# The recurrent layers' inputs and outputs kept on the chip instead of passed through transposed DRAM tensors

## The chip, the cores and the metric

One core of one Trainium2 chip runs the whole program. Its engines, as the profile names them, are PE (TensorE matmuls; PEld are its weight loads), DVE (VectorE), ACT (ScalarE), POOL (GpSimd) and SP (SyncE, which here only issues DMA transfers). The metric is the device time of one launch in microseconds (us), lower is better.

## The reference

Four layers with residuals over x of 2048 rows by 576 columns. Layers 1 and 3 (A) are dilated sliding window attention; layers 2 and 4 (B) are a recurrent attention with a memory of 8 rows that is handed from one segment of 32 rows to the next.

```
x = x + A(layernorm(x)); x = x + B(layernorm(x), mem0)
x = x + A(layernorm(x)); x = x + B(layernorm(x), mem0)

A: qkv = x @ wqkv (32 heads of 18); logits over the rows s, s-2, ..., s-14; softmax; @ wo
B: for each of 64 segments: h = [mem (8 rows), x segment (32 rows)]
     q, k, v = h @ Wq, Wk, Wv          (32 heads of 128)
     o = softmax(q k^T * scale, masked) v;  o = o @ Wo
     mem = o[:8]; output rows = o[8:]
```

## The kernel before

Activations are held transposed: 576 columns on 128 partitions in five chunks, rows along the free axis. Layer A works on tiles of T = 64 rows (32 tiles per layer, `a_tile`), layer B on segments of 32 rows. The two B layers advance together: step t (`b_step`) computes segment t of layer 2 (lane 0) and segment t - 6 of layer 4 (lane 1) in one tile hT of 96 columns, 80 of them used: 32 rows of lane 0, 2 x 8 rows of memory, 32 rows of lane 1. There are 70 steps, and two steps use up one A tile of layer 1 and one of layer 3.

A step on PE: projections q and k (L728/L730, eleven groups of up to three heads), v (L759, three blocks of 32 rows, two halves of 20 matmuls each), scores in two kinds, m (memory rows) and x (segment rows) (L790/L800), probabilities times v (L817 for m, L850 for x), output projection into the PSUM tile psY (L874, eight pieces of 20 matmuls). The memory rows of psY go at once into the next step's hT (`mem_out`, L893 to L895). The x rows of step t are projected one step later, together with the memory rows of step t + 1.

An A tile on PE: layernorm sums (L402), qkv in 15 blocks of 5 matmuls (L479), logits (L528), probabilities spread over the columns (L552: 16 matmuls, then 4 more into the same PSUM tile once it is empty), output in 5 blocks of 5 (L587). A block of A's weights is loaded from DRAM into one of six `ring` buffers (L423), 40 blocks in two steps.

PSUM: three tiles r for everything narrow, one tile o4 (spread and probabilities times v), one psY.

How data passed between the layers in the kernel before: the normalised A output (xnb) was stored by SP to xn2T or xn4T (L611), and per step a 32 row piece of each was loaded into hT (L704). The x rows of psY were copied to stg (L905), stored per lane to d2T or d4T (L911), and later loaded as dl (L451, L621) beside the residual x1T or x3T (L450, L620), added on DVE (L456 for layer 3's input, L625 for the final output), and for the output transposed on PE (L634) and stored (L645).

The order of the work is set by a planner (`_Plan.run`): each operation has engines it may run on, an estimated duration, a priority (lower first) and buffers it acquires; whenever an engine is free in the planner's clock it takes the ready operation of lowest priority number. The result is one fixed order of instructions per engine. Each engine executes its own in that order, waiting where a semaphore says so; SP issues its transfers in order too, so that a transfer which waits holds all behind it.

Of the kernel before, what the change touches and what calls it, by code (L numbers as in the profile page):

```python
# [16 lines left out]
P = 128  # L17
# [177 lines left out]
class _K:  # L195
# [37 lines left out]
    def setup(self):  # L233
# [5 lines left out]
        NT, NSEG = self.NT, self.NSEG  # L239
        self.x1T = dp.tile([P, NT, 5, T], F32, name="x1T")  # L240
        self.x3T = dp.tile([P, NT, 5, T], F32, name="x3T")
        self.xnT = [dp.tile([P, NSEG, 6, SEG], BF16, name=f"xn{l}T") for l in (2, 4)]
        self.dT = [dp.tile([P, NSEG, 5, SEG], F32, name=f"d{l}T") for l in (2, 4)]
# [113 lines left out]
        tiles("stg", 2, [P, 2, 5, SEG], F32)  # L357
        tiles("nmx", 4, [P, 8], F32)
        tiles("sum", 4, [P, 8], F32)
        tiles("xT", 3, [P, 5, T], F32)  # L360
        tiles("dl", 1, [P, NS, 5, SEG], F32)
# [14 lines left out]
        tiles("xnb", 2, [P, NS, 6, SEG], zero=True)  # L376
# [49 lines left out]
    def a_tile(self, layer, j, dep, due, span):  # L426
# [6 lines left out]
        xT = pl.buf("xT")  # L433
        if layer == 1:
            x0, ps = pl.buf("x0"), pl.buf("r")
            a = pl.op("SP", 0.5, lambda e: nc.sync.dma_start(out=x0.t[0:T, 0:D], in_=self.A_x[0, j * T:(j + 1) * T, :]),
                      pr(0), [dep], acq=[x0])

            def tr(e, ps=ps):
                for c in range(5):  # L440
                    nc.tensor.matmul(ps.t[:, c * T:(c + 1) * T], lhsT=x0.t[:, c * P:(c + 1) * P], rhs=self.ident[:, 0:T],
                                     start=True, stop=True)
            b = pl.op("PE", 0.16, tr, pr(0.04), [a], acq=[ps, xT], uses=[x0])
            o_x = pl.op(AD_, _evac(320), lambda e, ps=ps: self.copy(e, xT.t[:], ps.t[:, 0:5 * T].rearrange("p (c t) -> p c t", c=5)),
                        pr(0.05), [b], uses=[ps, xT])
        else:
            dl = pl.buf("dl")

            def ld(e):
                nc.sync.dma_start(out=xT.t[:], in_=self.x1T[:, j])  # L450
                nc.sync.dma_start(out=dl.t[:], in_=self.dT[0][:, NS * j:NS * j + NS])  # L451
            a = pl.op("SP", 1.0, ld, pr(0), [dep, self.x1_stored[j], *self.d_stored[0][NS * j:NS * j + NS]], acq=[xT, dl])

            def add(e):
                xv = xT.t[:].rearrange("p c (s n) -> p c s n", n=SEG)
                nc.vector.tensor_tensor(out=xv, in0=xv, in1=dl.t[:].rearrange("p s c n -> p c s n"), op=ALU.add)  # L456
            o_x = pl.op("DVE", 0.52, add, pr(0.05), [a], uses=[xT, dl])
# [138 lines left out]
        xnb = pl.buf("xnb")  # L596

        def wr2(e, m, rstd):
# [5 lines left out]
            for o, i, bc in views:  # L604
# [6 lines left out]
        o = pl.op("SP", 0.5, lambda e: nc.sync.dma_start(out=self.xnT[lane][:, NS * j:NS * j + NS], in_=xnb.t[:]),  # L611
                  pr(0.95), [o], uses=[xnb])
        self.xn_stored[lane][j] = o

    def finish_out(self, j, prio):
        nc, pl = self.nc, self.pl
        xT, dl, xb, ot = pl.buf("xT"), pl.buf("dl"), pl.buf("fin"), pl.buf("ot")

        def ld(e):
            nc.sync.dma_start(out=xT.t[:], in_=self.x3T[:, j])  # L620
            nc.sync.dma_start(out=dl.t[:], in_=self.dT[1][:, NS * j:NS * j + NS])  # L621
        a = pl.op("SP", 1.0, ld, prio, [self.x3_stored[j], *self.d_stored[1][NS * j:NS * j + NS]], acq=[xT, dl])

        def add(e):
            nc.vector.tensor_tensor(out=xb.t[:, 0:5 * T].rearrange("p (c s n) -> p c s n", c=5, n=SEG),  # L625
                                    in0=xT.t[:].rearrange("p c (s n) -> p c s n", n=SEG),
                                    in1=dl.t[:].rearrange("p s c n -> p c s n"), op=ALU.add)
        a = pl.op("DVE", 0.52, add, prio, [a], acq=[xb], uses=[xT, dl])
# [66 lines left out]
    def load_x(self, t):  # L695

        nc, pl = self.nc, self.pl
        hT = pl.buf("hT")
        self.hT[t] = hT
        segs = [(l, self.lane_seg(t, l)) for l in range(2) if self.lane_seg(t, l) is not None]  # L700

        def ld(e):
            for l, s in segs:
                nc.sync.dma_start(out=hT.t[:, :, XC[l]:XC[l] + SEG], in_=self.xnT[l][:, s])  # L704
        o = pl.op("SP", 0.5 * len(segs), ld, t - 0.42, [self.xn_stored[l][s // NS] for l, s in segs] + [self.qk_op.get(t - 1)],
                  acq=[hT])
        self.x_in[t] = o
        for l, s in segs:
            if s == 0:
                m0 = MC + l * NM  # L710
                o = pl.op("DVE", 0.2, lambda e, m0=m0: nc.vector.tensor_copy(out=hT.t[:, :, m0:m0 + NM], in_=self.mem0T[:]),
                          t - 0.4, [o], uses=[hT])
                self.mem_in.setdefault(t, []).append(o)

    def qk(self, t, g, prio):
# [16 lines left out]
        o = pl.op("PE", 0.358 * n, mm, prio, [self.x_in[t], *self.mem_in[t]], acq=[ps, sb], uses=[hT], tmin=TW[0])  # L732
# [9 lines left out]
    def vpass(self, t, b, prio):  # L742
# [5 lines left out]
        gate = pl.op("NONE", 0.0, None, prio, [self.x_in[t]], acq=[V])  # L748
        for r in range(2):
# [10 lines left out]
            o = pl.op("PE", 1.08, mm, prio, [self.x_in[t], gate] + (self.mem_in[t] if b == 1 else []), acq=[ps], uses=[hT, V],  # L760
# [121 lines left out]
    def mem_out(self, t, dep, prio):  # L882
# [13 lines left out]
        o = pl.op("DVE", 0.56, cp, prio, [dep, self.x_in[t + 1]], uses=[psY, hT])  # L896
        self.mem_in.setdefault(t + 1, []).append(o)

    def x_out(self, t, dep, prio):

        nc, pl, psY = self.nc, self.pl, self.psY
        if t < 0:
            return
        st = pl.buf("stg")
        o = pl.op(AD_, _evac(320), lambda e: self.copy(e, st.t[:].rearrange("p l c n -> p c l n"),  # L905
                                                       psY.t[:, :, 16:W80].rearrange("p c (l n) -> p c l n", l=2)),
                  prio, [dep], acq=[st], uses=[psY])
        for lane in range(2):
            s = self.lane_seg(t, lane)
            if s is not None:  # L910
                self.d_stored[lane][s] = pl.op("SP", 0.5, lambda e, lane=lane, s=s: nc.sync.dma_start(out=self.dT[lane][:, s], in_=st.t[:, lane]),  # L911
                                               prio, [o], uses=[st])
# [29 lines left out]
    def trace(self):  # L942
# [3 lines left out]
        self.xn_stored = [[None] * NT, [None] * NT]  # L946
        self.d_stored = [[None] * NSEG, [None] * NSEG]
        self.hT, self.x_in, self.mem_in, self.qk_op, self.V, self.v_ev, self.e_ = {}, {}, {}, {}, {}, {}, {}
        nl = 0
        for t in range(self.nsteps):  # L950
            while nl < NT and NS * nl <= t + LEAD:
                self.a_tile(1, nl, self.qk_op.get(t - 1), NS * nl - 0.5, 3.0)
                nl += 1
            for lane in range(2):
                s = self.lane_seg(t - 2, lane) if t >= 2 else None
                if s is not None and s % NS == NS - 1:
                    j = s // NS
                    if lane == 0:
                        self.a_tile(3, j, None, NS * j + self.dly - 0.5, 2.2)
                    else:  # L960
                        self.finish_out(j, t + 1.5)
            if t == 0:
# [75 lines left out]
```

## Time and profile before

| | before |
|---|---|
| time, median of 3 runs (range) | 2752.93 us (2750.78 to 2760.56) |
| the profiled execution: own time, span | 2747.74 us, 2745.9 us |
| granted TensorE clock, mean | 0.98 |
| busy: PE, DVE, ACT, POOL | 2388.5, 1927.1, 936.5, 980.0 us |
| DMA queue of SP: share of 16 engines | 35.9% (275.02 MB) |
| first PE instruction after the start of the span | 103.9 us (it waits for the first load of x) |

The span is cut by the profile in busy time and idle time of each engine, and idle time is put down to what ended it. A row such as "PE r L479 <- DMA ring<-wA_blk: 42.6, 57, 2.1" reads: PE, before matmuls of line 479 that write a tile r, sat idle 42.6 us in total in 57 places, at most 2.1 us, until a transfer into ring had landed.

### The profile page before, as it was taken

To read this page: it belongs to the slowest core of one execution; us is meant where nothing else is said; L and a number is where in the kernel's file an instruction comes from. 1 tells how busy PE (TensorE), PEld (TensorE's weight loads), DVE (VectorE), ACT (ScalarE), POOL (GpSimd) and SP (SyncE) were. 2 spreads that over 40 slices of the span, in tenths; PEclk is the share of its full clock that TensorE was granted. 3 is DMA by queue.
4 is the path that set the end of the run, shared out by engine and by line. 5 is a ranking of instruction groups with operands and counts; after the bars stand their busy time and mean duration, and the time that the engine had idled before them with its cause. 6 is when DMAs were issued, how large, how long until landed. Compare 5 with 4: busy or idle time off the path is not lost. (4 is left out here: it accounts for less than half of the span.)

```text
span 2745.9 us, 159278 instructions
## 1 busy us (share of the span) xinstructions
PE 2388.5 (87%) x73360; PEld 2001.8 (73%) x73360; DVE 1927.1 (70%) x4021; ACT 936.5 (34%) x2070; POOL 980.0 (36%) x1177
## 2 busy tenths in 40 slices
PE   0289999999989988999998989899999999999998
PEld 0177777777777777777777777777777777777777
DVE  1266777777777777777777777777777777776665
ACT  0023334333333333333333333333333333333322
POOL 3231333433434443334343344443433433332110
PEclk9999999999999999999999999999999999999999
DMA  7722433344443344334444434443334444432210
GB/s 253 198 74 65 117 103 104 108 115 118 117 126 110 108 124 115 104 98 122 123 115 123 125 100 117 126 113 109 110 108 127 111 123 127 118 86 79 64 30 19
DMA packets 368642, 304.08 MB, mean 111 GB/s; under 512 B 146788, under 2 KB 364452, under 8 KB 366436
## 3 DMA queue, kind: packets, MB, share of 16 engines
q1 hardware_dynamic: 364724, 275.02, 35.9%
q0 software_dynamic: 3248, 18.88, 2.0%
q8 instruction: 573, 9.39, 1.5%
q14 instruction: 97, 0.79, 0.1%
HBM read 260.88 MB, written 32.90 MB: 107 GB/s over the span
## 5 line engine op out<-in xcount | busy, mean ns | idle before, releaser
L728 PE MATMUL r<-hT,wq 128*128 128x80 bf16 x8960 | 694.5, 202 | 11.5 <-DVE V L225 6.2
L728 PE MATMUL r<-hT,wk 128*128 128x80 bf16 x8960 | 693.9, 202 | 0.0
L728 PEld LDWEIGHTS <-wq 128*128 128x128 bf16 x8960 | 463.8, 100 | 48.7 <-issue 45.2
L874 PE MATMUL psY<-OT,wo 128*128 128x80 bf16 (+1 forms) x11360 | 482.4, 208 | 18.7 <-ACT OT L223 9.4
L225 DVE CAST qk<-r 128x480 bf16<-128x480 f32 (+1 forms) x506 | 324.4, 642 | 242.2 <-PE r L730 219.6
L759 PE MATMUL r<-wv,hT 128*32 128x512 bf16 x6720 | 447.3, 384 | 51.6 <-ACT em L673 21.1
L874 PEld LDWEIGHTS <-wo 128*128 128x128 bf16 x11360 | 460.2, 104 | 30.3 <-issue 23.9
L728 PEld LDWEIGHTS <-wk 128*128 128x128 bf16 x8960 | 465.3, 100 | 0.1
L730 PE MATMUL r<-hT,wk_r 128*128 128x80 bf16 x2240 | 452.7, 202 | 0.0
L730 PE MATMUL r<-hT,wq_r 128*128 128x80 bf16 x2240 | 452.6, 202 | 0.0
L230 POOL TENSOR_TENSOR big<-qT,kT 128x1024 bf16<-128x1024 bf16 (+1 forms) x192 | 332.0, 1737 | 186.6 <-ACT kT L223 178.4
L759 PEld LDWEIGHTS <-hT 128*32 128x32 bf16 x8400 | 208.9, 97 | 229.8 <-issue 73.4
L230 POOL TENSOR_TENSOR ex<-ex,sum 128x384 bf16<-128x384 bf16 x140 | 117.0, 836 | 536.1 <-DVE sum L681 482.5
L479 PE MATMUL r<-xn,ring 128*128 128x64 bf16 x4800 | 235.3, 196 | 62.5 <-DMA ring<-wA_blk 50.5
L479 PEld LDWEIGHTS <-ring 128*128 128x128 bf16 x4800 | 179.7, 99 | 123.1 <-DMA ring<-wA_blk 76.1
L223 ACT ACTIVATE V<-r 128x512 bf16<-128x512 f32 x269 | 160.8, 598 | 289.3 <-PE r L759 289.0
L230 POOL TENSOR_TENSOR big<-big 128x1280 bf16<-128x1280 bf16 (+1 forms) x84 | 187.5, 2232 | 130.5 <-DVE big L230 128.5
L730 PEld LDWEIGHTS <-wq_r 128*128 128x128 bf16 x2240 | 224.1, 100 | 1.4 <-issue 1.3
L730 PEld LDWEIGHTS <-wk_r 128*128 128x128 bf16 x2240 | 224.1, 100 | 0.0
L223 ACT ACTIVATE qk<-r 128x480 bf16<-128x480 f32 (+1 forms) x264 | 146.7, 558 | 204.0 <-PE r L730 197.0
L223 ACT ACTIVATE OT<-o 128x512 bf16<-128x512 f32 (+1 forms) x299 | 143.1, 500 | 154.7 <-DVE OT L225 92.2
L223 ACT ACTIVATE big<-o 128x512 bf16<-128x512 f32 x220 | 125.1, 596 | 168.1 <-PE o L552 112.8
(137 smaller groups left out, 3643.7 us busy)
## 6 DMA issues: line engine op xcount, KB each, us to landing
ring<-wA_blk SPq DMA_DIRECT2D x1280, 160.0 KB, 3.2
x1T<-xT SPq DMA_DIRECT2D x32, 160.0 KB, 2.7
d2T<-stg SPq DMA_DIRECT2D x64, 80.0 KB, 3.2
xT<-x1T SPq DMA_DIRECT2D x32, 160.0 KB, 3.7
dl<-d2T SPq DMA_DIRECT2D x32, 160.0 KB, 4.3
x3T<-xT SPq DMA_DIRECT2D x32, 160.0 KB, 3.2
d4T<-stg SPq DMA_DIRECT2D x64, 80.0 KB, 3.0
xT<-x3T SPq DMA_DIRECT2D x32, 160.0 KB, 3.8
```

Source lines behind the costliest of these rows:

```text
L223: nc.scalar.activation(out=out, in_=in_, func=ACT.Copy, scale=1.0 if scale is None else scale)
L225: (nc.vector if e == "DVE" else nc.gpsimd).tensor_copy(out=out, in_=in_)
L230: (self.nc.vector if e == "DVE" else self.nc.gpsimd).tensor_tensor(out=out, in0=in0, in1=in1, op=op)
L479: nc.tensor.matmul(ps.t[:, c * T:(c + 1) * T], lhsT=w.t[:, kc, :], rhs=xn.t[:, kc, :], start=(kc == 0), stop=(kc == 4))
L728: nc.tensor.matmul(pv[:, hh, wi, :], lhsT=wt[:, kc, h * P:(h + 1) * P], rhs=hT.t[:, kc, 0:W80], start=(kc == 0), stop=False)
L730: nc.tensor.matmul(pv[:, hh, wi, :], lhsT=wr[:, (h % 16) * P:(h % 16 + 1) * P], rhs=hT.t[:, 4 + h // 16, 0:W80], start=False, stop=True)
L759: nc.tensor.matmul(ps.t[c * 32:(c + 1) * 32, :], lhsT=l, rhs=w, start=(kc == 0), stop=(kc == 4))
L874: nc.tensor.matmul(psY.t[:, mb, c0:], lhsT=self.wo[:, w0:w0 + P], rhs=self.OT[:, h, c0:], start=(h == 0 and mb == 0), stop=(h == NH - 1 an ...
```

## The change

Four edits, and a new order that follows from them.

- `load_x`: no transfer. hT's x columns are copied from xnb on POOL or DVE (128 copies of 128 x 192 elements). xnb has its own two buffers per layer.
- `x_out`: no copy to stg and no store. DVE adds psY's rows of a lane straight to the residual tile, which `residual` has loaded before: in place for layer 3's input (tile x3), into `fin` for the final output (tile x5 is loaded, fin is written).
- `a_tile` for layer 3 and `finish_out` begin with those tiles and load nothing; the two DVE additions of 64 rows fall away.
- Priorities: A tiles of layer 1 are due at 2*nl - 0.6 with a spread of 3.5 (was - 0.5, 3.0), those of layer 3 at 2*j + 4.8 with 1.0 (was 2*j + 5.5 with 2.2).

```
 load_x:
-        def ld(e):
-            for l, s in segs:
-                nc.sync.dma_start(out=hT.t[:, :, XC[l]:XC[l] + SEG], in_=self.xnT[l][:, s])
+        gate = pl.op("NONE", 0.0, None, t - 0.42, [self.qk_op.get(t - 1)], acq=[hT])
+            xnb, dep = self.xn_ready[l][s // NS]
+            self.x_in[t][l] = pl.op(("POOL", "DVE"), (0.45, 0.2),
+                                    lambda e, ...: self.copy(e, hT.t[:, :, XC[l]:XC[l] + SEG], xnb.t[:, s % NS]),
+                                    t - 0.42, [dep, gate], uses=[hT, xnb])
 new:
+    def residual(self, lane, j, dep, prio):
+        b = pl.buf(("x3", "x5")[lane])
+        xb = pl.buf("fin") if lane == 1 else None
+        src = (self.x1T, self.x3T)[lane]
+        o = pl.op("SP", 0.5, lambda e: nc.sync.dma_start(out=b.t[:], in_=src[:, j]), prio, ...
 x_out:
-        st = pl.buf("stg")
-        o = pl.op(AD_, _evac(320), lambda e: self.copy(e, st.t[:]..., psY.t[:, :, 16:W80]...), ...)
-                self.d_stored[lane][s] = pl.op("SP", 0.5, lambda e, ...: nc.sync.dma_start(out=self.dT[lane][:, s], in_=st.t[:, lane]), ...)
+                x = xT.t[:, :, w]
+                o = x if xb is None else xb.t[:, 0:5 * T]...[:, :, w]
+                nc.vector.tensor_tensor(out=o, in0=x, in1=psY.t[:, :, c0:c0 + SEG], op=ALU.add)
 trace:
-                self.a_tile(1, nl, self.qk_op.get(t - 1), NS * nl - 0.5, 3.0)
+                self.a_tile(1, nl, self.qk_op.get(t - 1), NS * nl - 0.6, 3.5)
-                        self.a_tile(3, j, None, NS * j + self.dly - 0.5, 2.2)
+                        self.a_tile(3, j, None, NS * j + self.dly - 1.2, 1.0)
+            for lane in range(2):
+                s = self.lane_seg(t, lane)
+                if s is not None and s % NS == 0:
+                    self.residual(lane, s // NS, self.qk_op.get(t - 1), t + 0.3)
```

Instructions by engine, before and after: PE 146722 rows both times, line for line the same number of matmuls; SP 1894 and 1510 issues (gone are 128 stores of d2T/d4T, 64 loads of dl, 64 stores and 128 loads of xn2T/xn4T); DVE 4023 and 4096; ACT 2072 and 2050; POOL 1182 and 1255. The planner also gives some operations to another engine: the widest addition of an A tile (128 x 1280 elements) goes 58 times to POOL and 6 times to DVE before, 5 and 59 times after; 90 evacuations of q and k go from DVE to ACT.

Both orders repeat every two steps through the middle of the program, here called the even and the odd step of a pair. PE in the order after, odd step, from the end of its output projection: 16 spread matmuls (L542), one transpose of `fin` (L622), the first q/k group of the next step, three weight blocks of an A tile (L469), then probabilities times v (L841, into o4), one block, the two halves of v, the last 4 spread matmuls, five blocks and more. Even step: m scores, x scores, layernorm sums (L401), half of v, logits (L518), half of v, two q/k groups, 16 spread matmuls, A's output (L577), one q/k group, 4 spread matmuls. In the order before, the even step has m scores, x scores and both halves of v in a row, and its spread stands among the output projection: 16 spread matmuls, 20 of L874, layernorm sums, 4 spread matmuls, probabilities times v (L817).

SP's queue at the turn from an even to an odd step. Ahead of the fence: in the order before, x3T, xT, dl and xn2T stand between the ring loads that follow an A tile's output and the next ones.

```order
L423 DMA ring_335<-wA_blk 128x640
L423 DMA ring_336<-wA_blk 128x640
L593 DMA x3T<-xT_303 128x320
L450 DMA xT_302<-x1T 128x320
L451 DMA dl_305<-d2T 128x320
L611 DMA xn2T<-xnb_325 128x384
L423 DMA ring_331<-wA_blk 128x640
```

The same turn in the order after, where x_298 is a tile x3 and x_300 the tile x5:

```order
L422 DMA ring_334<-wA_blk 128x640
L609 DMA x_298<-x1T 128x320
L422 DMA ring_335<-wA_blk 128x640
L422 DMA ring_330<-wA_blk 128x640
L422 DMA ring_332<-wA_blk 128x640
L422 DMA ring_331<-wA_blk 128x640
L422 DMA ring_333<-wA_blk 128x640
L422 DMA ring_334<-wA_blk 128x640
L609 DMA x_300<-x3T 128x320
L422 DMA ring_335<-wA_blk 128x640
```

Two residual loads are left at this turn, six ring loads apart.

DVE in the even step, at the softmax of the first scores (nmx is a negated maximum, sum a row sum, em the m probabilities, st the layernorm statistics), before:

```order
L670 TENSOR_REDUCE nmx_294<-r_340 128x4
L671 TENSOR_TENSOR r_340<-r_340,nmx_294 128x320
L670 TENSOR_REDUCE nmx_295<-r_342 128x8
L671 TENSOR_TENSOR r_342<-r_342,nmx_295 128x384
L680 TENSOR_REDUCE sum_298<-em_268 128x4
L681 RECIPROCAL sum_298<-sum_298 128x4
L683 TENSOR_TENSOR em_268<-em_268,sum_298 128x4x80
```

And after:

```order
L658 TENSOR_REDUCE nmx_288<-r_339 128x4
L659 TENSOR_TENSOR r_339<-r_339,nmx_288 128x320
L407 TENSOR_SCALAR st_304<-r_340 128x64
L408 TENSOR_TENSOR st_304<-st_304 128x64
L409 SCALAR_TENSOR_TENSOR st_304<-r_340,st_304 128x64
L668 TENSOR_REDUCE sum_292<-em_264 128x4
L669 RECIPROCAL sum_292<-sum_292 128x4
L671 TENSOR_TENSOR em_264<-em_264,sum_292 128x4x80
L658 TENSOR_REDUCE nmx_289<-r_341 128x8
L659 TENSOR_TENSOR r_341<-r_341,nmx_289 128x384
```

Three statistics of a layernorm and the m normalisation now stand ahead of the x scores' maximum, which before followed the m maximum directly.

DVE at the end of the odd step's output projection, after (`big` is the A tile's spread tile, OT the B heads' output):

```order
L884 CAST hT_260<-psY 128x4x16
L885 CAST hT_260<-psY 64x16
L886 CAST hT_260<-psY 64x16
L225 CAST big_314<-o_342 128x32x16 x2
L906 TENSOR_TENSOR x_299<-x_299,psY 128x5x32
L230 TENSOR_TENSOR big_314<-big_314,vT_309 128x1024 x2
L225 CAST OT<-o_342 128x2x4x64
L906 TENSOR_TENSOR fin_327<-x_300,psY 128x5x32
```

The memory copies come first, then two of the four evacuations of the spread tile, and the two new additions (L906) stand between products of A and an evacuation of B.

More of the change, by code (lines that the diff above doesn't have):

```diff
@@ L375, in setup @@
         tiles("oT", 1, [P, 5, T])
-        tiles("xnb", 2, [P, NS, 6, SEG], zero=True)
+        tiles("xnb1", 2, [P, NS, 6, SEG], zero=True)
+        tiles("xnb3", 2, [P, NS, 6, SEG], zero=True)
         tiles("fin", 1, [P, 6 * T], zero=True)
@@ L446, in a_tile @@
         else:
-            dl = pl.buf("dl")
-            def ld(e):
[L450 to L457, printed above, removed]
+            xT = self.acc[0][j][0]
+            o_x = self.x_done[0][NS * j + NS - 1]
         xn = pl.buf("xn")
@@ L595, in a_tile @@
         (self.x1_stored if layer == 1 else self.x3_stored)[j] = xst
-        xnb = pl.buf("xnb")
+        xnb = pl.buf(f"xnb{layer}")
         def wr2(e, m, rstd):
@@ L895, in cp @@
             nc.vector.tensor_copy(out=hT.t[64:128, 5, MC + a:MC + b], in_=y[0:64, 4, a:b])
-        o = pl.op("DVE", 0.56, cp, prio, [dep, self.x_in[t + 1]], uses=[psY, hT])
+        o = pl.op("DVE", 0.56, cp, prio, [dep, self.gate[t + 1]], uses=[psY, hT])
         self.mem_in.setdefault(t + 1, []).append(o)
```

73 lines of the change are left out of this document (34 added, 39 removed).

## The prediction

> **What bounds the kernel now.** I read the page's totals first, then the steady part of the program cut out by windows, then what ended PE's idle time there, then the places themselves on the timeline. The first two rows are the page's: the span, and each engine's busy time. The last is a window (start and end, length, then busy time and instructions of PE, PEld, DVE, ACT and POOL, granted clock, DMA share, GB/s).
>
> ```profile
> span 2745.9 us, 159278 instructions
> PE 2388.5 (87%) x73360; PEld 2001.8 (73%) x73360; DVE 1927.1 (70%) x4021; ACT 936.5 (34%) x2070; POOL 980.0 (36%) x1177
> ...
> 480.00:2320.00 1840.00, 1677.48 (x51662) 1406.42 (x51663) 1378.78 (x2853) 676.58 (x1507) 730.93 (x828) 0.98 0.41 115
> ```
>
> PE is the bound: 91% busy from 480 to 2320 us (1677.48 of 1840), at a clock of 0.98, so nothing is to be had from the clock. The change leaves PE its 146722 rows. It can therefore move only PE's idle time: 1840 - 1677.48 = 162.5 us in this stretch, which is 24.4 pairs of steps of 75.3 us. The waits name who ended it (total us, times, longest); the last two rows are from 2320 us to the end.
>
> ```profile
> PE r L479 <- DMA ring<-wA_blk: 42.6, 57, 2.1
> PE o L552 <- ACT big L223: 36.0, 24, 1.5
> PE o L817 <- ACT big L223: 18.1, 24, 0.8
> PE r L759 <- DVE st L410: 15.9, 24, 0.7
> PE r L759 <- ACT em L673: 15.1, 37, 0.9
> PE o L850 <- issue: 8.5, 10, 1.5
> PE r L728 <- DVE V L225: 5.8, 14, 0.4
> ...
> PE psY L874 <- ACT OT L223: 7.9, 8, 1.8
> PE r L634 <- DVE fin L625: 4.9, 1, 4.9
> ```
>
> No row says that PE waits for hT's x rows, or for dl and xT. The DRAM round trips which the edits remove are hidden, but for one at the very end (4.9). What they do is hold up SP's queue, and the queue brings A's weights: 42.6 us. The other large terms are the single tile o4 (36.0 + 18.1) and the three tiles r (15.9 + 15.1 + 5.8).
>
> **Ring waits.** The queue of SP at the turn of a pair, and what SP's largest waits there were (before a row's transfer can start):
>
> ```profile
> 1236.51 0.38 SPq L593 DMA_DIRECT2D x3T<-xT  x1
> 1237.32 0.32 SPq L450 DMA_DIRECT2D xT<-x1T  x1
> 1237.69 0.44 SPq L451 DMA_DIRECT2D dl<-d2T  x1
> 1239.99 0.32 SPq L611 DMA_DIRECT2D xn2T<-xnb  x1
> 1240.40 2.30 SPq L423 DMA_DIRECT2D ring<-wA_blk  x5
> ...
> SPq L645 <- ACT ot L223: 262.7, 24, 11.6
> SPq L911 <- ACT stg L223: 170.1, 24, 8.3
> ```
>
> From 1236.51 to 1240.40 no ring load is issued: 3.9 us, of which L450, L451 and L611 with their waits take 1240.40 - 1237.32 = 3.1. L911 holds the queue 170.1 / 24 = 7.1 us a pair. All of these issues go (384 fewer on SP). L645 stays, with its 10.9 us a pair; 64 residual loads come, two issues of about 0.4 us (by L450's 0.32 and L451's 0.44) for 16 removed. One of the two may wait for its tile; in the new order six ring loads stand behind it that PE needs some 25 us later. Bounds: nothing gained, if L645 and the six buffers were the cause, to the whole 42.6. I take 36, five sixths, since nothing but L593 and the residuals is left between the loads at the turn. **-36** (0 to -42.6).
>
> **The tile o4.** One even step in the order before, PE rows (start, length, line; in brackets the idle time just before and who ended it):
>
> ```profile
> 1221.14 0.40 PE L552 MATMUL o<-e,epadT 32*128 32x128 bf16 x16
> ...
> 1224.15 0.24 PE L552 MATMUL o<-e,epadT 32*128 32x128 bf16 x4 [1.50 <-ACT big L223]
> 1225.14 0.53 PE L817 MATMUL o<-ptm,V 32*128 32x16 bf16 x48 [0.76 <-ACT big L223]
> ```
>
> The 16 spread matmuls end at 1221.54, the last 4 can start at 1224.15: four evacuations on ACT and DVE take 2.6 us, of which PE covers about 1.1 with 20 matmuls of the projection and layernorm sums. Then 0.76 for the 4. A pair pays (36.0 + 18.1) / 24.4 = 2.2 us. In the new order the sequence stands twice in a pair, since layer 3's tile and layer 1's now spread in different places. At the turn from odd to even, one transpose, one q/k group and three blocks lie behind the 16 spread matmuls, about 1.7 us, and then L841 needs o4: 2.6 - 1.7 = 0.9 exposed. The even step has L577's 25 matmuls and one q/k group, about 1.5 us: 1.1 exposed, and 0.1 for the 4 after it. Sum 2.1 a pair against 2.2: **-3** (-20, were the covers 0.4 longer each, to +10, were they 0.2 shorter each).
>
> **The tiles r and the softmax.** The timeline at an even step's scores:
>
> ```profile
> 1206.69 0.32 PE L800 MATMUL r<-qk 128*32 128x80 bf16 x16
> ...
> 1208.33 0.44 ACT L673 ACTIVATE em<-r 128x320 bf16<-128x320 f32 x1 [3.33 <-DVE r L671]
> 1208.82 1.05 PE L759 MATMUL r<-wv,hT 128*32 128x512 bf16 x16 [0.20 <-ACT em L673]
> 1248.78 1.05 PE L759 MATMUL r<-wv,hT 128*32 128x512 bf16 x16 [0.86 <-ACT em L673]
> ```
>
> The tile of the m scores is full at 1207.01 and free when em is read out, at 1208.8: 1.8 us. In between PE had x scores and half of v (1.26 us), and waited 0.20. In the new even step only layernorm sums (some 0.6 us) stand after the x scores: about 0.8 exposed. The x scores' own maximum moves behind the layernorm's statistics on DVE, so their tile comes free later too, which the second half of v pays in part. I put this at 2.0 us a pair against (15.9 + 15.1 + 5.8) / 24.4 = 1.5: **+12**. Bounds: 0, if the statistics run while PE is busy with logits, to +45, which is the price of one long statistics instruction a pair (below).
>
> **Second layernorm and the first q/k group after the projection.** Layer 1's and layer 3's layernorm sums now stand apart; the one among the projection waits for squares from ACT or POOL. And in two places a pair the next thing PE does after the projection needs the memory rows:
>
> ```profile
> 1186.55 3.03 PE L874 MATMUL psY<-OT,wo 128*128 128x80 bf16 x80
> ...
> 1189.93 0.17 DVE L895 CAST hT<-psY 64x16 bf16<-64x16 f32 x1
> ```
>
> From the end of psY (1189.58) to the end of L895 (1190.10) is 0.52 us. The 16 spread matmuls cover 0.40 of it in the odd case; the rest is 0.12 to 0.2 a pair, so +4. With +5 for the layernorm (0.2 a pair, a guess between nothing and the 0.65 that L410 costs each time now: 15.9 / 24): **+9** (0 to +20).
>
> **The copies of hT, and who pays for what leaves.** What DVE, POOL and ACT gain or lose, by groups (busy us, mean ns):
>
> ```profile
> L230 POOL TENSOR_TENSOR big<-big 128x1280 bf16<-128x1280 bf16 x58 | 151.2, 2606 | 128.5 <-DVE big L230 128.5
> L489 POOL COPY kT<-halo 128x70 bf16<-128x70 bf16 x62 | 16.6, 267 | 0.0
> L223 ACT ACTIVATE stg<-psY 128x320 f32<-128x320 f32 x68 | 29.6, 435 | 194.1 <-PE r L479 106.4 <-PE psY L874 35.4 <-DVE hT L895 35.2
> L225 DVE CAST qk<-r 128x480 bf16<-128x480 f32 x462 | 302.9, 656 | 235.0 <-PE r L730 216.2 <-PE r L634 12.2 <-PE r L479 1.2
> ...
> L590 DVE TENSOR_TENSOR xT<-xT,r x64: 436/477/489, 132.2 to 2640.2; 128x320 f32<-128x320 f32 x64
> L625 DVE TENSOR_TENSOR fin<-xT,dl x32: 449/952/958, 489.2 to 2740.8; 128x320 bf16<-128x320 f32 x32
> ```
>
> A copy of 192 elements is nearest to L489's of 70 (267 ns): I estimate 0.5 us on POOL, 95 x 0.5 = 47 us. POOL loses 53 additions of 2.6 us (138 us) and gets some smaller ones from DVE: less busy than before. DVE gets 128 additions of 160 elements (about half of L590's 477 ns for 320: 0.24 to 0.3, so 35 us) and those 53 wide ones at 0.83 (44); it gives up 90 casts at 656 ns (59), L456 (32 at L590's 477 ns, 15), L625 (32 x 0.952, 30), and some smaller ones: about even. ACT loses 68 x 0.435 = 30 and gains the casts: even. All three stay under PE. The copy stands a step before its use, since xnb is ready when the A tile is: cost 0. The additions hold psY longer than the copy to stg, by at most two queued pieces of A (under 2 us), but the next projection starts some 30 us later: 0. Without these covers the copy would cost 128 x 0.5 = 64 us at most.
>
> **The ends.** The start, up to the first q/k groups, has the same order on PE: 0. Between 2320 and 2610 us the waits for OT (7.9) lose their place, but new ones for ring and o4 come: **-3** (-10 to +3). The very end is the chain that ended last:
>
> ```profile
> 2736.46 0.50 DVE stg L225
> 2736.97 1.58 DMA d4T<-stg
> 2738.57 2.12 DMA dl<-d4T
> 2740.79 0.50 DVE fin L625
> ```
>
> The 4.8 us from 2736.46 to 2741.29, from the end of the last projection to PE's transposes, become one addition of 160 elements: **-4.5** (-4 to -5).
>
> Sum: -36 - 3 + 12 + 9 - 3 - 4.5 = -25.5. The profiled span of 2745.9 becomes 2720, its own time of 2747.74 becomes 2722; the median of the runs, 2752.93, lies 5.2 above that, so I say 2727.
>
> **Rivals.** First, no change: the gain at the ring is real, but what PE saves there it waits for elsewhere, for with three tiles r and one o4 the softmax and the evacuations run on DVE and ACT at their own pace. The r term is then at its upper end: -36 - 3 + 45 + 9 - 3 - 4.5 = +7.5, about 2760. For it: PE's waits at L759 move by whole microseconds with one evacuation (0.20 and 0.86 above). Against: ACT is 37% busy and DVE 75% in the stretch (676.58 and 1378.78 of 1840), so they can catch up.
>
> Second, slower: DVE instructions that are held while POOL works. The rows of the two (min, median, max in ns):
>
> ```profile
> L409 DVE TENSOR_TENSOR st<-st x128: 224/758/2599, 106.9 to 2646.0; 128x64 f32<-128x64 f32 x128
> L683 DVE TENSOR_TENSOR em<-em,sum x140: 491/492/2199, 160.6 to 2723.6; 128x320 bf16<-128x320 bf16 x140
> ```
>
> 64 elements take 224 ns at best and 2599 at worst, and 2.6 us is also what POOL's wide addition takes. In the new even step L409 and L683's form stand between the m scores' maximum and the x scores' maximum, with PE behind them. One held 2599 - 758 = 1.84 us in each pair costs 24.4 x 1.84 = 45 us: with -25.5 that is +19.5, so 2772; if the em product is held as well, by 2199 - 492 = 1.71, another 42, so 2814. I name 2780. To be slower at all the hold has to beat 25.5 us, 1.05 a pair, and 1.6 a pair ((25.5 + 13.8) / 24.4) to be 0.5% slower. Against it: only 5 of the wide additions stay on POOL, so its long instructions, which do the holding, go; and the median of L683 equals its minimum.
>
> [...]
>
> Third, more gain: the waits put down to issue (8.5 and others) and the layernorm's 15.9 go as well, since A's tiles stand further from the softmax: another 35 to 45 us, 2682 to 2692. For it: both rows exist, and the new priority numbers move just these. Against: nothing in the order removes a use of r. That the round trips are not removed at all is excluded by the issues that are missing from SP.
>
> **Numbers.** The forecast with its neighbours (2690 to 2739) 0.50, no change 0.24, slower 0.18, more gain 0.08. About 0.5%, 14 us, is what a measurement here can tell from nothing: 2739 to 2767. Faster is then the forecast and more gain, 0.58. The range from 2680 to 2770 leaves out most of the slower case and the far end of the gain.
>
> **What the profile after would show.** Ring waits under 10 us between 480 and 2320 (if over 25, L645 or the buffers were the cause). Waits for ACT's big before L542 and L841 near 50 in sum. Waits of L750 and L401 for em and st near 50; if they stand at 80 or more and L409's counterpart has a median over 1 us, the second rival holds. No DMA in the last chain after psY, and L906 near 0.3 us. Wrong I would be above all if idle time that I count by tile turns out to pass from one tile to the next, so that taking one wait away only feeds another.

## The result, and the profile after

The kernel after takes 2676.78 us (median of 4 runs, 2674.42 to 2678.57), the kernel before in the same comparison 2756.74 us. The ratio is 0.9707 with a 95% interval of 0.9677 to 0.9737: 2.9% faster. The forecast was 2727 in a range from 2680 to 2770. The direction was right; the gain is about three times the forecast's, and falls just below the range.

The page's totals after, and then a window row for the same stretch of steps in each kernel, from the end of step 9 to the end of step 59, which is 25 pairs: first before, then after.

```profile
span 2673.1 us, 158511 instructions
...
PE 2348.8 (88%) x73360; PEld 1975.7 (74%) x73360; DVE 1783.3 (67%) x4094; ACT 942.6 (35%) x2048; POOL 913.2 (34%) x1250
```

```profile
505.50:2393.80 1888.30, 1721.63 (x52962) 1443.65 (x52955) 1416.10 (x2925) 696.07 (x1550) 751.10 (x848) 0.98 0.41 115
```

```profile
510.80:2340.60 1829.80, 1687.26 (x52943) 1419.40 (x52942) 1278.67 (x2976) 710.58 (x1549) 680.63 (x898) 1.00 0.36 104
```

The span is 72.8 us shorter, and it splits in two. PE's idle time fell from 2745.9 - 2388.5 = 357.4 to 2673.1 - 2348.8 = 324.3, that is by 33.1. PE's busy time fell by 39.7, with exactly the same 73360 matmuls. Work that is the same and takes less time ran at a higher clock: the granted clock of the whole span is 0.994 against 0.980. In the 25 pairs the split is 24.1 idle (1888.30 - 1721.63 = 166.7 to 1829.80 - 1687.26 = 142.5) and 34.4 busy (1721.63 to 1687.26); the steps after them give 19.6 us more, the first ten steps are 5.3 longer.

PE's waits after, 480 to 2320 us:

```profile
PE o L841 <- DVE big L225: 29.1, 25, 1.2
PE r L750 <- ACT em L661: 28.5, 50, 0.9
PE o L542 <- DVE big L225: 19.7, 25, 0.8
PE o L841 <- issue: 12.5, 12, 2.1
PE r L469 <- DMA ring<-wA_blk: 12.5, 21, 2.2
PE r L750 <- ACT V L223: 10.4, 25, 0.4
PE psY L865 <- issue: 7.1, 15, 1.7
```

Ring is 12.5 (42.6 before), o4 29.1 + 19.7 = 48.8 (54.1), the tiles r 28.5 + 10.4 = 38.9 (36.8), and the layernorm's row of 15.9 is gone. The rows put down to issue have grown: all of them together from 22.3 to 32.4 us.

In the trace's clock record of the 25 pairs before, a stretch of half clock lasts 3.413 us 22 times and 6.827 us twice. Where the clock went is seen in windows of 3.41 us, around the even step's spread of before (the place that the prediction showed, at 1221 us), and around the odd turn's spread of after. Columns as above: PE busy is the second number behind the times, the clock the third from the end.

```profile
1217.79:1221.21 3.42, 3.42 (x110) 3.21 (x100) 3.22 (x10) 2.03 (x6) 0.00 (x0) 1.00 0.18 34
1221.21:1224.62 3.41, 1.68 (x46) 1.35 (x46) 3.05 (x7) 2.17 (x5) 0.83 (x1) 1.00 0.84 272
1224.62:1228.03 3.41, 2.89 (x82) 2.82 (x82) 3.38 (x5) 1.21 (x3) 2.19 (x1) 0.50 0.07 21
1228.03:1231.45 3.42, 3.42 (x55) 3.42 (x52) 1.54 (x3) 0.60 (x2) 2.02 (x3) 0.50 0.00 0
1231.45:1234.86 3.41, 3.07 (x145) 2.19 (x143) 2.34 (x7) 1.96 (x4) 0.72 (x1) 1.00 0.18 52
```

```profile
1168.51:1171.92 3.41, 2.75 (x83) 2.55 (x80) 1.40 (x5) 1.47 (x4) 1.17 (x4) 1.00 0.02 5
1171.92:1175.33 3.41, 2.91 (x133) 1.99 (x136) 3.01 (x7) 1.29 (x3) 0.00 (x0) 1.00 0.71 203
1175.33:1178.75 3.42, 3.36 (x96) 2.83 (x85) 2.99 (x6) 1.78 (x4) 0.27 (x1) 1.00 0.41 114
```

Before, the wait of 1.50 us and the first 0.23 of the wait of 0.76 fall into the second window, PE is busy for 1.68 of its 3.41 us, and in the next two windows the clock is 0.50. After, the same kind of wait, 1.16 us, stands alone and is cut in two by a window's edge: its windows are busy for 2.75 and 2.91 us, and the clock stays at 1.00. Whole in one window it would leave PE busy for 0.66 of it. Counted in the trace's clock record over the 25 pairs, 26 windows are at half clock before and 5 after; between 480 and 2320 us 19 of the 23 times that the clock halved in before followed this place. Each loses half of its 3.41 us of clock, 1.7 us: 44.4 us against 8.5, which is 35.9 of clock beside the 34.4 of busy time that the 25 pairs lost.

All starts of half clock in that record lie a whole number of 3.413 us apart, within one execution (29 starts in before and 8 in after, to within 0.01 us). So the time can be cut into such windows and PE's share of each measured. Over nine executions of the kernels of this study, in their 25 pairs, of the windows at full clock with PE busy for less than 0.45 of the time 57 of 57 are followed by a half clock window, of those from 0.45 to 0.50 27 of 37, from 0.50 to 0.60 25 of 87, from 0.60 to 0.65 3 of 76, and above 0.65 none of some 4500. In the executions of before and after alone these are 16 of 16, 4 of 5, 8 of 25, 1 of 22 and none of 986. The ends of matmuls are modelled in the profile, so the shares are not sharp, and between 0.45 and 0.65 they do not decide alone.

### The profile page after: what moved, and what is told of

The parts are those of the page before. It is cut to its first block, busy times and chain, and to the rows that moved or that the text cites. A ratio compares the mean times of both kernels' runs of the same rounds, so it can differ in the third digit from the quotient of the medians.

```text
span 2673.1 us, 158511 instructions
## 1 busy us (share of the span) xinstructions
PE 2348.8 (88%) x73360; PEld 1975.7 (74%) x73360; DVE 1783.3 (67%) x4094; ACT 942.6 (35%) x2048; POOL 913.2 (34%) x1250
## 4 chain that ended last, share of the span: by engine, by line
PE 67%; DVE 11%; ACT 7%; DMA 6%; issue 3%; SPq 3%; POOL 2%; ACTq 0%; DVEq 0%; POOLq 0%
PE r L718 21%; PE r L750 14%; PE psY L865 12%; DMA ring<-wA_blk 6%; PE r L720 5%; PE r L469 5%; DVE big L225 3%; ACT big L223 3%; PE o L841 2%; SPq L298 2%; ACT OT L223 2%; PE o L808 2%; DVE r L659 2%; DVE nmx L658 1%; PE o L542 1%
## 5 line engine op out<-in xcount | busy, mean ns | idle before, releaser
L718 PEld LDWEIGHTS <-wq 128*128 128x128 bf16 x8960 | 461.4, 100 | 36.8 <-issue 33.2
L865 PE MATMUL psY<-OT,wo 128*128 128x80 bf16 (+1 forms) x11360 | 451.7, 202 | 19.4 <-issue 8.2
L865 PEld LDWEIGHTS <-wo 128*128 128x128 bf16 x11360 | 428.4, 100 | 29.1 <-issue 27.0
L225 DVE CAST qk<-r 128x480 bf16<-128x480 f32 (+1 forms) x409 | 262.6, 642 | 259.4 <-PE r L720 256.3
L230 POOL TENSOR_TENSOR big<-qT,kT 128x1024 bf16<-128x1024 bf16 (+1 forms) x192 | 326.0, 1705 | 140.2 <-ACT kT L223 48.6
L223 ACT ACTIVATE qk<-r 128x480 bf16<-128x480 f32 (+1 forms) x361 | 200.7, 557 | 182.6 <-PE r L720 181.9
L469 PE MATMUL r<-xn,ring 128*128 128x64 bf16 x4800 | 237.4, 196 | 26.0 <-DMA ring<-wA_blk 18.0
L223 ACT ACTIVATE OT<-o 128x512 bf16<-128x512 f32 (+1 forms) x335 | 163.3, 507 | 243.0 <-PE o L841 101.5
L230 POOL TENSOR_TENSOR big<-big 128x640 bf16<-128x640 bf16 (+1 forms) x62 | 93.1, 1501 | 417.5 <-DVE big L230 407.4
L469 PEld LDWEIGHTS <-ring 128*128 128x128 bf16 x4800 | 181.5, 99 | 66.9 <-issue 33.3
L223 ACT ACTIVATE V<-r 128x512 bf16<-128x512 f32 x250 | 149.2, 597 | 208.5 <-PE r L750 206.8
L750 PE MATMUL r<-wv_r,hT 128*32 128x512 bf16 x1680 | 169.7, 382 | 0.8 <-issue 0.8
```

What stands on the lines that cost most here:

```text
L223: nc.scalar.activation(out=out, in_=in_, func=ACT.Copy, scale=1.0 if scale is None else scale)
L225: (nc.vector if e == "DVE" else nc.gpsimd).tensor_copy(out=out, in_=in_)
L230: (self.nc.vector if e == "DVE" else self.nc.gpsimd).tensor_tensor(out=out, in0=in0, in1=in1, op=op)
L469: nc.tensor.matmul(ps.t[:, c * T:(c + 1) * T], lhsT=w.t[:, kc, :], rhs=xn.t[:, kc, :], start=(kc == 0), stop=(kc == 4))
L718: nc.tensor.matmul(pv[:, hh, wi, :], lhsT=wt[:, kc, h * P:(h + 1) * P], rhs=hT.t[:, kc, 0:W80], start=(kc == 0), stop=False)
L750: nc.tensor.matmul(ps.t[c * 32:(c + 1) * 32, :], lhsT=l, rhs=w, start=(kc == 0), stop=(kc == 4))
```

## Experiments: is it the clock?

Theory A says that some 40 us of the gain are the clock, lost before because two waits shared a window. To test it without moving anything else, PE gets unused matmuls in the gap of 1.50 us; the wait for o4 stays, and only PE's idleness in it goes.

```
 layernorm:  (fill = 24 or 8 for layer 1's first layernorm, else 0)
                                  rhs=xs.t[:, c]..., start=(c == 0), stop=(c == 4))
+            for _ in range(fill):
+                nc.tensor.matmul(ps.t[:, 256:256 + P], lhsT=self.ones[:, :], rhs=self.ident[:, :], start=True, stop=True)
```

> The kernel before with 24 matmuls of 128 x 128 that nothing uses, about 1.4 us, put right behind the layernorm sums of layer 1, where PE idles 1.50 us in each pair before the last 4 spread matmuls; 32 x 24 matmuls more, nothing else moves. Theory A (of the 77 us, about 40 are the TensorE clock, which halves for 3.4 us after a 3.4 us window in which PE was busy under about 55%; before, the two waits of 1.50 and 0.76 us fall into one such window in most pairs): the idle time there goes, the halved windows at that place go with it, the lost clock time falls from 57 us to 15 to 25, and the kernel is 30 to 40 us faster, near 2718, although it does more work. Theory B (the clock in before is low for another reason, such as the 13% more DMA traffic or DVE's 8% more work, and the gain at that place is the idle time itself): the clock stays near 0.98, and the time is the same or up to 10 us longer.

> The same with 8 matmuls, about 0.46 us: the busy share of the window with both waits rises from 0.34 to about 0.47. Theory A: that is still under the limit of about 0.55, so most halved windows at that place stay (only those where the waits were split by a window's edge go), lost clock 35 to 55 us, time 0 to 20 us shorter than before. If a half filled wait were worth a third of what the 24 give, the clock would follow the share without a limit. Theory B: no change of the clock.

> Control for the fill of 24: the same 24 unused matmuls a pair in the kernel before, but behind the other layernorm of the same tile, one place later, where PE does not wait: the waits of 1.50 and 0.76 us stay. Theory A: the halved windows stay (35 to 50 us lost between steps 10 and 60), the work of 32 x 1.4 = 44 us comes on top, less what other waits absorb: 2770 to 2795. Theory D (any extra PE work raises the clock, the place does not matter): lost clock under 20 us and 2730 to 2755.

Measured against the kernel before: 24 in the gap 0.9947 (0.9922 to 0.9972), 8 in the gap 0.9996 (0.9975 to 1.0017), 24 outside the gap 1.0114 (1.0078 to 1.0149). The window rows of the 25 pairs, for 24, 8, and 24 elsewhere:

```profile
517.80:2376.40 1858.60, 1726.08 (x53552) 1446.39 (x53553) 1416.36 (x2925) 694.01 (x1550) 752.50 (x848) 0.99 0.42 117
```

```profile
507.00:2389.30 1882.30, 1728.09 (x53153) 1446.93 (x53152) 1417.11 (x2925) 695.95 (x1550) 752.36 (x848) 0.98 0.42 115
```

```profile
513.00:2414.20 1901.20, 1742.48 (x53551) 1468.18 (x53552) 1415.39 (x2925) 696.21 (x1550) 751.09 (x848) 0.98 0.41 114
```

With 24 in the gap the 25 pairs take 1858.6 us against 1888.3, although PE does 600 matmuls more: 6 windows at half clock instead of 26. Its busy time rises by only 4.5 us for work that takes 600 x 56 ns = 34 us back to back at full clock (spacing of 128 column matmuls in the trace). With 8 there are 21 such windows, and with 24 elsewhere 18, at 12.9 us more than before. Counted by place: of 24 times that the clock halved in before 20 followed the even step's spread, with 24 in the gap none of 5, with 24 elsewhere 16 of 18. That bears out A and excludes B, since DMA traffic (0.41 to 0.42 of the time) and DVE's work are the same in all of them, and D, since the place decides. The control's 18 in place of 26 come from the shortest of its four runs; over all four the clock of the whole span is 0.978 on average, and 0.979 in before on the same chip. The 8 also agree with A: the fill raised the share of a window with both waits from 0.34 to between 0.43 and 0.49, and of the windows counted above 57 of 57 under 0.45 and 27 of 37 from 0.45 to 0.50 were followed by half clock. The row of the wait shows that it was filled:

```profile
PE o L554 <- ACT big L223: 4.0, 25, 0.2
```

The whole run gained only half of what the 25 pairs gained, 2733.6 against 2749.37 us, and not the 30 to 40 expected. In the profiled execution the first ten steps are 12.3 us longer (517.8 against 505.5). The rows of the start (the fill first) show a clock of 0.74 with the fill and 1.00 in before:

```profile
104.00:190.00 86.00, 57.93 (x1252) 49.20 (x1255) 44.94 (x93) 18.92 (x44) 28.08 (x38) 0.74 0.45 127
```

```profile
104.00:180.00 76.00, 48.85 (x1161) 39.13 (x1164) 44.32 (x92) 18.00 (x43) 25.69 (x36) 1.00 0.49 143
```

That 1.00 is not a full clock. In before the trace's clock record begins only at 149.4 us, and time without a record counts as 1.00. The layernorm sums show the clock instead: the first row is from 104 to 150 us, the second from 1000 to 1300, both in before.

```profile
L402 PE MATMUL r<-xs,ones 128*128 128x128 bf16 x16 | 2.4, 306 | 6.9 <-DVE xs L396 6.9
L402 PE MATMUL r<-xs,ones 128*128 128x128 bf16 x60 | 6.2, 230 | 0.0
```

They start mostly 107 ns apart there and 56 ns apart later, as these matmuls do inside and outside the half clock stretches of this trace's record. So the start is slow in both kernels, and the fill adds work to it: 168 of the unused matmuls fall into the first ten steps, 96 of them 107 ns apart and 72 at 56, in all 14.3 us.

## Experiments: which part of the change brings it?

```
 before_newprio: the kernel before with   NS * nl - 0.6, 3.5   and   NS * j + self.dly - 1.2, 1.0
 after_oldprio:  the kernel after with    NS * nl - 0.5, 3.0   and   NS * j + self.dly - 0.5, 2.2
 xout_only:      the kernel after with before's load_x, xnT and the store L611
```

> The kernel after with the two priority lines of before; its PE order in a pair is that of before, with 16 spread matmuls, layernorm sums and 4 spread matmuls in the middle of the output projection. No DRAM round trips. Theory A: the ring waits go as in after (under 16 us), but the halved windows stay, 35 to 55 us of lost clock, so it gains the idle part alone: 2710 to 2730. Theory B: the edits themselves, not the order, bring the clock back, since DMA and DVE have less to do: 2675 to 2690 with a clock of 0.99.

> The kernel before with the two priority lines of after and nothing else; all DRAM round trips stay. Question: are the priorities alone worth the gain? With the round trip of d2T in between, layer 3's tile cannot start when its new due time asks for it; in the planned order nearly all of both A tiles falls into one step of the pair (50 matmuls of L587 in a row, 45 of L479, spread 20 in a row), the other step has almost none. Theory A (the additions from PSUM are what lets the new due times be kept): not faster than before, 2750 to 2850, ring waits well over 42 us since 40 weight blocks are asked for in one step. Theory C (the priority numbers carry the gain, the edits are only cleaner): 2680 to 2710.

> The kernel after with load_x of before: hT's x columns come by the DRAM round trip (xn2T, xn4T, 64 stores and 128 loads), the outputs are added from psY; new priorities, and PE's order in a pair is word for word that of after. Theory A: clock as in after (0.99). The ring waits lie between after's 12.5 us and before's 42.6; at 20 the time is 2685, range 2675 to 2700. If the SP queue's round trips of hT's input were what cost the ring, it stands near 2705. Theory B: with two thirds of the removed transfers back, a clock nearer to 0.98, and 2700 to 2720.

| kernel | additions from psY | hT copied | priorities | ratio to before (interval) |
|---|---|---|---|---|
| after | yes | yes | new | 0.9707 (0.9677 to 0.9737) |
| xout_only | yes | no | new | 0.9747 (0.9712 to 0.9782) |
| after_oldprio | yes | yes | old | 0.9937 (0.9912 to 0.9961) |
| before_newprio | no | no | new | 1.3253 (1.3218 to 1.3288) |

Neither part does it alone. With all round trips gone but the old due times, 2734.33 us are left, a little over the expectation, which had ring waits under 16 us and 35 to 55 us of lost clock; they were 24.1 and 71.7. The 25 pairs and the largest waits:

```profile
506.70:2393.30 1886.60, 1732.46 (x52958) 1464.02 (x52953) 1433.85 (x3100) 641.01 (x1450) 753.18 (x873) 0.96 0.35 101
```

```profile
PE o L542 <- DVE big L225: 61.4, 25, 2.5
PE r L469 <- DMA ring<-wA_blk: 24.1, 38, 1.8
PE psY L865 <- ACT OT L223: 13.2, 25, 0.5
```

DMA has less to do than in before (0.35 against 0.41), and the clock is worse, 0.96: 42 windows at half clock. Nothing but five layernorm matmuls stands between the 16 and the 4 spread matmuls there, and the gap is 2.46 us in one piece. So here the clock followed the order and not the traffic. The gap can be filled here too, with 40 unused matmuls:

> The kernel after with the old priorities, and 40 unused matmuls (about 2.3 us) behind the layernorm sums of layer 1, where PE idles 2.46 us in each pair before the last 4 spread matmuls. Theory A: the lost clock time between steps 10 and 60 falls from 72 us to under 20, and the time by 35 to 55 us, to 2680 to 2700, less some 10 us for the tiles of the start, where the extra matmuls fall into no gap. Theory B (clock follows traffic or another load): no change, or up to 20 us longer by the extra work.

It ran in 2716.66 us, ratio 0.9895 (0.9848 to 0.9942), 18 us less than without the fill though on another chip (by the ratios 0.4% or 12 us, and the intervals overlap), and less than expected. In the 25 pairs the outcome is as A says: 4 windows at half clock, 1848.2 us against 1886.6, so 38 shorter; the start is 16 us longer, where 280 of the unused matmuls fall.

```profile
522.90:2371.10 1848.20, 1741.09 (x53953) 1476.81 (x53953) 1437.05 (x3100) 641.57 (x1450) 752.90 (x873) 1.00 0.35 103
```

The new priorities on the kernel before are far worse than the 2750 to 2850 us expected, at 3636.92 us:

```profile
570.50:3295.90 2725.40, 1846.81 (x53071) 1509.16 (x53068) 1495.00 (x3203) 628.17 (x1382) 619.64 (x780) 0.81 0.29 80
```

```profile
PE r L479 <- DMA ring<-wA_blk: 250.3, 117, 3.5
PE r L587 <- DMA ring<-wA_blk: 152.0, 69, 3.4
PE r L528 <- POOL big L230: 108.5, 65, 5.1
PE r L587 <- DVE oT L230: 73.4, 26, 5.2
```

Both A tiles fall into one step, the ring waits reach 400 us, and the clock is halved in long stretches (0.81 on average). So the due times alone gain nothing here. That they need layer 3's residual input to be ready at once is the expectation's reason, which this outcome fits.

xout_only has the PE order of after, and its clock (3 windows at half). Its ring waits:

```profile
PE r L470 <- DMA ring<-wA_blk: 19.0, 30, 1.5
```

So in the new order the 192 issues of hT's round trip hardly hold the ring: with them back, 19.0 us, and 12.4 in a second run, against 12.5 in after and 42.6 in before. The copy on chip was timed once more beside after:

> The kernel after once more, beside the next three on the same chip: 2670 to 2685, lost clock between steps 10 and 60 under 15 us.

> hT's x columns still by DRAM, all else as after: 0 to 8 us longer than after, since its ring waits were 20.5 us against 13.6.

On that chip after takes 2667.07 us, 0.9712 (0.9688 to 0.9735), and xout_only 2677.09, 0.9757 (0.9734 to 0.978): all four runs of after lie below all six of xout_only, and the difference is 0.4% to 0.5% of before in both comparisons, 10 to 12 us, a little over the expected 0 to 8; the intervals overlap in the first and just touch in the second. The 25 pairs take 1830.6 us in the profiled execution of the first xout_only and 1829.8 in that of after, so there the difference lies at the ends.

Which of L911 and the dl loads held the ring in the old order was not separated; in after_oldprio, without either, 24.1 us remain. One more wait went with the order and not with the edits. In before, apart from the ring loads' own waits for a free buffer, SP's queue stood longest at the store of the output (L645, 262.7 us). This store is L633 in the two kernels without dl; SP's wait for it from 480 to 2320 us, in after_oldprio and then in after:

```profile
SPq L633 <- ACT ot L223: 260.2, 24, 11.1
SPq L633 <- ACT OT L223: 0.2, 1, 0.2
```

How much of the ring's 24.1 to 12.5 us is this, and how much the more even demand of the new order, stays open.

## Experiment: one evacuation in place of four

The trace of after shows the four evacuations of the spread tile one after the other on two engines (each row's bracket names the other engine as what it waited for):

```profile
1169.69 0.60 ACT L223 ACTIVATE big<-o 128x512 bf16<-128x512 f32 x1 [1.70 <-POOL kT L479]
1170.32 0.69 DVE L225 CAST big<-o 128x512 bf16<-128x512 f32 x1 [0.54 <-ACT big L223]
1171.05 0.60 ACT L223 ACTIVATE big<-o 128x512 bf16<-128x512 f32 x1 [0.76 <-DVE big L225]
1171.68 0.69 DVE L225 CAST big<-o 128x512 bf16<-128x512 f32 x1 [0.66 <-ACT big L223]
```

```
-        for g in range(NQ):
-            evs.append(pl.op(AD_, _evac(512), ... big.t[:, 0:4, :, g * 16:(g + 1) * 16] <- ps.t[:, g, :] ...
+        evs.append(pl.op("ACT", 1.7, lambda e, ps=ps: self.copy(e, big.t[:, 0:4].rearrange("p c w (g t) -> p g (c w) t", g=NQ),
+                                                                ps.t[:].rearrange("p g (m t) -> p g m t", t=16)), ...
```

> The kernel after, but the spread tile is evacuated by one ACT instruction over all four banks (128 x 2048) in place of four of 512 on ACT and DVE, which in the trace run strictly one after the other (0.60, 0.69, 0.60, 0.69, in all 2.6 us). From the rows of 256 and 512 elements (383 and 597 ns) one of 2048 takes about 1.9 us. PE's two waits for o4 behind it, 29.1 + 19.7 us and most of the 12.5 put down to issue, shrink by about 0.7 us each in a pair: 25 to 35 us shorter, 2640 to 2655, the clock stays at 0.99. If the four were serial only because ACT and DVE were busy with other things, the one instruction would be no shorter a chain, and q/k evacuations queued behind it on ACT would cost: 2675 to 2695.

> The kernel with one evacuation of 2048 elements, beside the kernel after: 12 to 22 us shorter than that.

> Between the two: the spread tile is evacuated by two instructions of 1024 elements, on ACT and DVE as the planner likes. They still run one after the other, about 1.05 and 1.2 us, so the chain is 2.3 us and not 1.9, but neither engine is held for 1.9 us. If the q/k waits that the long instruction brought (33 us before L717) are what it gave back, this one has fewer of them and lands within 8 us of it on either side; if the length of the chain is all that counts, it gains 5 to 10 us over after: 2665 to 2672.

The one instruction takes 1876 ns, as expected. It ran in 2657.66 us (ratio 0.9689), and beside after on one chip in 2659.36 against 2667.07, ratios 0.9682 (0.9657 to 0.9706) and 0.9712 (0.9688 to 0.9735). That is 8 us or 0.3%, not the 25 to 35 expected first nor the 12 to 22 expected next, and the intervals overlap. The waits show where the rest went:

```profile
PE r L717 <- DVE qk L225: 33.3, 25, 1.8
PE r L749 <- ACT em L660: 30.1, 50, 1.0
PE o L840 <- issue: 11.5, 13, 1.6
...
PE r L717 <- ACT qk L223: 7.9, 22, 0.4
```

Of the 29.1 and 19.7 us before L841 and L542 only 5.6 are left, and in their place PE waits 33.3 + 7.9 us for a tile r until a q/k evacuation is done, most of it on DVE. That DVE is late because ACT is held for 1.9 us is likely, but not shown. Two instructions of 1024 take 2665.88 us, 0.9708 (0.9678 to 0.9738), level with after. There the q/k waits are gone, but 26.9 + 15.4 us of the waits for o4 stay and 17.9 us for a layernorm statistic come; the time fits both of the expectation's outcomes, so it does not decide between them. The version with one evacuation is the fastest that was run, by a margin that these runs do not settle.

## Why the prediction was right or wrong, point by point

**The step that failed** is in the first part: "at a clock of 0.98, so nothing is to be had from the clock". The 2% of that row were 26 windows at half clock in the 25 pairs, most of them tied to one place. The prediction put that place at 2.2 us a pair, as idle time; with a half clock window behind it in 19 of the stretch's 24 pairs it cost up to 1.7 more. The clock term was put at nothing in the sum; it was 39.7 us of busy time. Rows of single pairs, in windows of before, would have said so:

```profile
1190.24:1265.50 75.26, 68.87 (x2056) 57.16 (x2054) 56.15 (x114) 27.78 (x62) 30.04 (x34) 0.93 0.41 114
```

```profile
1458.90:1534.20 75.30, 67.61 (x2122) 56.43 (x2118) 56.52 (x117) 27.65 (x63) 30.07 (x34) 1.00 0.41 113
```

One pair has a mean clock of 0.93, another 1.00, in nearly the same work.

**Idle time.** Forecast -25.5, measured -33.1. That these are near is in part luck, for errors of both signs cancel. By terms:

- Ring -36: 42.6 went to 12.5, so -30. The size was about right. The reason given, that L450, L451 and L611 with their waits stand between the loads, holds at most for a part: with L611 back the waits stay low, and without any of the removed transfers but with the old order they are 24.1. "L645 stays, with its 10.9 us a pair" was wrong: its wait is there with the old order and gone with the new. The 16 removed issues a pair should be 14, 12 fewer when the two residual loads are counted; no term rests on it.
- o4 -3: 54.1 to 48.8, with "issue" before L841 rising from 8.5 to 12.5. Right, as idle time.
- The tiles r +12: 36.8 to 38.9, +2. The even step was costed too high: the wait for em is 28.5 / 25.1 pairs = 1.1 us and V's evacuation 0.4, in sum 1.5, against 2.0 forecast.
- Second layernorm and first q/k group +9: no row of either is left in this stretch; nothing came. What came instead was not costed: 10 us more put down to issue.
- The ends: the last addition is as forecast, 0.32 us in place of the DMA round trip, but the last ten steps gave 12.8 us idle where 7.5 were said, and 6.9 of clock.
- The start 0: it is 5.3 us longer, of which 3.7 idle.

```profile
2663.42 4.92 PE L865 MATMUL psY<-OT,wo 128*128 128x64 bf16 x160 [0.91 <-DVE OT L225]
2668.38 0.32 DVE L906 TENSOR_TENSOR fin<-x,psY 128x160 bf16<-128x160 f32 x1 [3.17 <-PE psY L865]
2668.76 0.45 PE L622 MATMUL r<-ident,fin 128*128 128x128 bf16 x5 [0.42 <-DVE fin L906]
```

**What was costed at nothing** stayed hidden: the copies of hT take 347 ns on POOL, not the 0.5 us estimated, the additions from psY 0.31 to 0.32, and no wait of PE is for either but for one of 0.4 us at the end.

```profile
L225 POOL COPY hT<-xnb 128x192 bf16<-128x192 bf16 x95 | 31.2, 347 | 16.5 <-DVE xnb L598 16.2 <-PE r L750 0.3
```

**The rivals.** No change fell: the r term is not at its upper end. Slower fell: the instruction that had 224, 758 and 2599 ns now has 224, 225 and 1054, and the em product keeps its median.

```profile
L408 DVE TENSOR_TENSOR st<-st x128: 224/225/1054, 106.0 to 2571.9; 128x64 f32<-128x64 f32 x128
L671 DVE TENSOR_TENSOR em<-em,sum x140: 491/491/1591, 161.1 to 2655.5; 128x320 bf16<-128x320 bf16 x140
```

Before, 87 of the 128 instructions of L409 took more than 1.3 times their 224 ns, and all 87 began while a POOL instruction ran and ended 78 to 83 ns after the end of one; after, 36 of 128 did. Of the 140 em products 58 were stretched so before, which ended 344 to 352 ns after the end of a POOL instruction, and 4 after. So the wide additions' move off POOL, named as the argument against that rival, took most of the holds away, as far as the trace shows; it was not tested alone. DVE's busy time, costed as about even, fell by 143.8 us, 79.9 of them at L409 (128.1 to 48.2 at L408 after) and 49.2 at the em product (120.8 to 71.6). More gain, given 0.08, comes nearest to the time with its 2682 to 2692, but for the wrong reason: the layernorm's 15.9 did go, yet the waits put down to issue grew.

## What to carry to other kernels

Cost a wait of a matmul-bound kernel twice: as its own idle time, and, together with the waits next to it, by the clock lost behind them: here a window of 3.41 us in which PE was busy for 1.68 was followed by half clock, and each 3.41 us of that cost 1.7, 44.4 us in the 25 pairs before. Look up the granted clock in narrow windows at the places with the largest waits before calling a mean of 0.98 nothing, and where a wait cannot go, put independent matmuls into it (24 in the gap: 6 windows at half clock in place of 26) or move it away from its neighbour (the order after: 5). And an edit that makes a result available earlier may be worth little by itself and much by the order that it allows; test the two apart.

## What was not expected of the hardware

- A window of 3.41 us with PE's gap of 1.50 us and 0.23 of the one of 0.76 was followed by 6.83 us at half clock; in the 25 pairs before the clock halved 24 times, 22 times for 3.41 us and twice for 6.83. In the 25 pairs of nine executions half clock followed every window at full clock with a busy share under 0.45 (57 of 57) and none above 0.65; in all fourteen executions, from the first record of the clock to the end, 2 of some 9700 windows above 0.65 were followed by half clock, at 0.70 and 0.71.
- The kernel before spreads from 2733.59 to 2764.84 us over 24 runs on one chip, with a granted clock from 0.974 to 0.983 that is mostly lower in the longer runs. The kernel after spreads from 2674.42 to 2678.57 over 4 runs on one and 2662.84 to 2670.95 over 4 on another, with 0.994 to 0.996. That the grid of 3.41 us lies differently against the steps in each execution, so that the waits share a window more or less often, would explain the spread of before; it was not tested.
- A clock of 1.00 in the trace's rows is no measurement before the first record of the clock: in before the matmuls until 149 us start 107 ns apart where 56 is full speed.
- Adding 600 unused matmuls in the middle of the program made its 25 pairs 29.7 us shorter.
